# Decayed attention and a gated convolution on one core: transposes in 64-row tiles, states in two column tiles, and a new order of steps

## The chip, the core and the metric

The kernel runs on one core of one Trainium2 chip. The metric is the device time of one execution in microseconds (us), as the median of several runs. TensorE (PE in the profile, its weight loads PEld), VectorE (DVE), ScalarE (ACT) and GpSimd (POOL) each run their own queue of instructions in order; SyncE (SP) issues most of the DMAs. The engines wait for each other by semaphores.

## What is computed

For 4 batches of 8 heads, 768 positions and head size 48, a complex decay runs along the sequence; its output, with the heads put side by side (384 columns), goes through a gate from a convolution of five taps and two matrix products. All is in float32.

```python
for t in range(S):
    new_re = ar * S_re - ai * S_im          # ar, ai: decay of step t, magnitude at most 0.999
    new_im = ar * S_im + ai * S_re
    S_re, S_im = new_re + k[t] (x) v[t], new_im
    y[t] = q[t] @ S_re
gate = sigmoid(sum over 5 taps of conv_w[k] * x[t - 4 + k])     # x: y of all heads
out = (gate * (x @ w_val)) @ w_out
```

## The kernel before

The kernel turns the recurrence into chunks of 128 positions. ScalarE and VectorE make the running sum of the logarithm of the decay and of its angle, and from these the products `kx` and `qx`: each key and query times cosine and sine of the angle and times a growing or shrinking factor, 96 columns a head. With them a chunk's output is a masked product of queries and keys inside the chunk, plus queries times the state that the chunks before have left.

The work is cut into nine units (`UNITS`): the first batch's first half in two parts of 2 and 6 heads, then a unit for every half (384 positions) of all 8 heads of a batch. What a unit goes through, with the letter of each step:

- `a` to `p`: the chain on ScalarE and VectorE that makes angles and factors. `q` makes the key product (two instructions on VectorE, L473 and L477; `kx` has one buffer), `r` the query product.
- `K` stores `kx` to DRAM (`kd`), `N` reads it back as `kn`, with positions on the partitions, for the states. Both are DMAs on SP's queue.
- `T` turns keys and queries on TensorE (L526): a matmul against the identity, three of 128 positions each for one head and half, into one PSUM bank. `U` copies a bank to `kT` or `qT` on ScalarE.
- `s` forms scores (L555 to L560), `M` masks them on VectorE (L571), `t` adds a chunk to the states (L593, 4 heads a step), `u` copies the states, `y` forms outputs (L628, L633, L638), `v` copies them (both copies on ScalarE), `X` moves them to `xT` by DMAs that GpSimd issues.
- `C` and `D` are the taps of the convolution (the first on ScalarE, four on VectorE, L691), `G` the gate on ScalarE, `P` the product with `w_val` (L722), `Z` gate times value on VectorE, `O` the product with `w_out` (L729), `Q` its copy on ScalarE, `W` the store.
- `j` and `l` are the offsets (L363, two matmuls of 384 columns in all), `w` and `L` the weights, `A` and `V` the loads, `B` a copy on GpSimd.

The table `ORDER`, a string of these letters, sets the order of all steps: the program calls the generators one letter after the other, and each instruction is tied behind the one before it on its engine. A float32 matmul runs as two passes, so the trace has twice the program's count of them; a transpose runs as one.

A matmul that writes only partitions 0 to 63 or 64 to 127 of a bank (scores: 64 weight columns; outputs: 48) takes a column tile of TensorE's array, and a matmul of the other half can go beside it. Transposes, states, offsets and `P` and `O` took the full array. Four PSUM banks (`mm`) serve `T`, `P`, `O`, `j` and `l`.

Behind the tiled part lies a step-by-step version of the recurrence, taken only when a flag says that the factors left the safe range; in these runs it isn't.

Of the kernel before, what the change touches and what calls it, by code (L numbers as in the profile page):

```python
# [10 lines left out]
F32 = mybir.dt.float32  # L11
# [14 lines left out]
BUFS = {'in': 4, 'v': 2, 'kn': 2, 'xT': 2, 'z': 2, 'lv': 2, 'an': 2, 'tmp': 2, 'qx': 2, 'kx': 1, 'kT': 6, 'S': 1, 'S_sb': 3, 'S_cr': 4, 'y_sb': 3, 'sm': 2, 'ot': 2, 'mm': 4, 'y': 1}  # L26
XSTEP = 2
PIN_SP = True
POOLQ = 'X'
TAP0 = 'act'  # L30
ORDER = (
    "AAVLaaAbcceafgadiibclmhhdcwjwwwhhjwkknpewpBfkkwwoVgqArowqriinooTTBAaAaUAlmpbUpTUqATUrKcdqTUTLwssANtr"
    "TaTTuAhMMyhacUjwUUbsvceyvkcMskseBfnKtugfMigTdiyvtuilwooilshympAAANtmvMuTThqUUqtujUUtuprMTrUTTtyTuVUU"
    "UTTTvysMpkUtvTpsMkUsTautaUyuAbUMTvTKUAqUAcywTTvyNcUUsesUMMsrvTntfXXyoouwvgUTMdTtyUUXvTTiUXutqBUAhATr"
    "AhiATwauyUwLUalmpjtsskTTpTvMMbUUsUywcMvkTTcUUwTUyvTXTunTewyUTTqUsTUUwvosoMsyrMwMXvXKNtuATTUfUyvqgBUX"
    "UrPituTXCDDTTtyUUKUuNasMstTTaUiulvDsUyCmXCMTCMtCvCCDPputypGZCUDACvuPtdhTTuhtUTUTCGybUUssjutPvkwXMysk"
    "wPGcuZZZdhtTMMnovoyTUTTZAAqOcrvyqhQXeUTTUTUTUTXXUTUUUTjvUsfAAsrMyaMsvkayMPukvyVOnboBvgcWZKUoNiilmXXX"
    "DXtDuTDCCCOUtQDWTTTDQTAAutUTUUUssDDUcOMWDDupTpMOOrtQTWQTyCCqGWUvsAQDuydMvTUUtuUTTTAAtUqKrhPhGGPyeaUU"
    "sTvjNaZTUMyfubZcgBkPPPkZviiltZXZVmssMydnooTAXpTMTutvyBchqWUTUTUTUTeUUUUTTTUfqOKsspMgMiivysvyhutQUUTr"
    "TTvUMTUlmuAyUUvssMyMrvpsMyvTTjUTTpUUUXXNtuXXkkTTTUtUunPZotuTTqTyBUUUssMMTToTvysvyqUUArrKNUUtuTUTTtuO"  # L40
    "vQXMyUUsvsMyMvsMyvTTtuTTUUUtuUTTtUTTTutUyUUssUXvCDMyvMsyCXCCuvTUMTTCCUUTUtWWPTTTUCyuCUUssXMMvyvCDDDD"
    "CsMyEPvOOQQXWWXOQWGZXXPPPGZGZZZPtODCOOuCDDDDDCCQWDDDDCZQWQWyGvXOQWPZGEEGOQWOQWOCQPPZDCZOOCCCGDQDDDWG"
    "QWXCCPZPPCCCGOZZOOOQWQWWQQWW"
# [9 lines left out]
def kernel(  # L53
# [233 lines left out]
    def mm():  # L287
        return ps.tile([P, 512], F32, name="mm", bufs=BUFS["mm"])
# [3 lines left out]
    def weights():  # L292
        cw_row = const.tile([TAPS * NT, P], F32, name="cw_row")
# [287 lines left out]
    def states():  # L581
        for i, (u, n, rs) in enumerate(chunks):
# [6 lines left out]
            for r in rs:  # L589
                for w in range(2):  # L590
                    h = r + w * (g // 2)
                    at = ((n % HN) * g + h) * C2
                    pe(nc.tensor.matmul(  # L593
                        S_ps[bank(u, rs)][:C2, (2 * (h0 + r) + w) * D:(2 * (h0 + r) + w + 1) * D], kn[:, at:at + C2],
                        v_b[b][:, head(u, h), n],
                        start=(i == firsts[bank(u, rs)] and r == rs[0] and w == 0), stop=(n == NCH - 2),
                        skip_group_check=True,
                    ))
# [226 lines left out]
    def step_by_step():  # L825
# [7 lines left out]
        with ExitStack() as es:  # L833
# [13 lines left out]
            with tc.For_i(0, S, TB) as t0:  # L847
                tl = {}
                for nm, src in (("ar", a_re), ("ai", a_im), ("k", k), ("q", q), ("v", v)):
# [56 lines left out]
                for b in range(B):  # L906
                    nc.sync.dma_start(
                        out=xd[b, ds(t0, TB), :].rearrange("t (h e) -> h t e", e=D), in_=yo[b * H:(b + 1) * H]
                    )
            with tc.For_i(0, B, 1) as b:  # L910
                xn = sp.tile([P, J, DM], F32, name="xn")
                nc.sync.dma_start(out=xn, in_=xd[ds(b, 1)].rearrange("o (p j) c -> (o p) j c", j=J))
# [13 lines left out]
                for t0 in (0, HS):  # L926
# [5 lines left out]
                    for m in range(t0, t0 + HS, P):  # L932
# [4 lines left out]
                        nc.sync.dma_start(out=out[ds(b, 1), m:m + P].rearrange("o p c -> (o p) c"), in_=ot)  # L937
# [32 lines left out]
```

## Time and profile before

| | before |
|---|---|
| median of 3 runs | 320.6 us (316.15 to 323.51) |
| profiled execution | 317.13 us |
| its span, from the first to the last instruction | 315.4 us |
| TensorE, VectorE, ScalarE busy | 275.7, 240.7, 239.1 us |
| TensorE's mean granted clock | 0.982 |

The span is what the trace covers; the execution is a little longer. Busy times are unions of the instructions' own times. Matmuls are pipelined: one takes about 0.25 us from start to end while others start behind it every 0.1 us, so busy is not the same as at its peak.

### The profile page before, as it was taken

The numbers are of one execution on the slowest core, as the hardware profiler recorded it, in microseconds if no ns is written. First come the engines' busy times: TensorE is split into PE (matmuls) and PEld (weight loads), VectorE is DVE, ScalarE is ACT, GpSimd is POOL, SyncE is SP. The second block draws the span as 40 slices with busy tenths as digits, with TensorE's granted clock in tenths as the row PEclk, the third lists the DMA queues.
The fourth block names the chain that finished last, engine by engine and source line by source line (L and its number), as shares of the span: only waits on it lengthen the run. The fifth ranks groups of instructions, "written<-read, shape, count | busy, mean of one in ns | idle before, by whom it ended". The sixth has DMA issues, their size and how long they took to land.

```text
span 315.4 us, 7175 instructions
## 1 busy us (share of the span) xinstructions
PE 275.7 (87%) x2887; PEld 211.5 (67%) x2887; DVE 240.7 (76%) x289; ACT 239.1 (76%) x429; POOL 63.4 (20%) x124
## 2 busy tenths in 40 slices
PE   0342959987899999999999999999998999999992
PEld 0121646876687888787778668898898875655551
DVE  4978989997999999999799996983823692281730
ACT  6999989998899999999999899579445515333211
POOL 6410001132017000643400302331333020030000
PEclk9999987997999999999999999999999999999999
DMA  7999999699579498998269698792582012042111
GB/s 185 197 261 316 331 208 172 216 267 279 147 253 224 181 237 214 194 226 240 57 191 271 238 211 146 239 231 60 188 189 72 22 38 77 0 137 76 52 48 58
DMA packets 73748, 54.80 MB, mean 174 GB/s; under 512 B 28511, under 2 KB 70766, under 8 KB 72814
## 3 DMA queue, kind: packets, MB, share of 16 engines
q1 hardware_dynamic: 71150, 49.57, 62.1%
q0 software_dynamic: 2560, 4.72, 6.2%
q8 instruction: 24, 0.39, 0.5%
q14 instruction: 14, 0.11, 0.1%
HBM read 35.40 MB, written 14.16 MB: 157 GB/s over the span
## 4 chain that ended last, share of the span: by engine, by line
PE 58%; ACT 17%; DVE 10%; DMA 9%; issue 2%; SPq 1%; POOL 0%; DVEq 0%; ACTq 0%; POOLq 0%
PE mm L722 14%; PE mm L729 14%; PE mm L526 8%; PE S_ps L593 5%; DMA kn<-kd 5%; PE y_ps L628 4%; DMA kd<-kx 3%; PE sc_ps L555 3%; DVE kx L477 3%; ACT tmp L147 3%; ACT L145 3%; ACT qx L147 2%; PE y_ps L633 2%; PE y_ps L638 2%; ACT lv L147 2%
## 5 line engine op out<-in xcount | busy, mean ns | idle before, releaser
L157 POOL DMA_DIRECT2D xT<-y_sb x80 | 40.3, 510 | 148.3 <-ACT y_sb L150 115.6
L691 DVE SCALAR_TENSOR_TENSOR z<-xT,cw_sb,z 128x768 f32<-128x768 f32 (+1 forms) x60 | 50.4, 862 | 8.3 <-ACT z L147 6.7
L722 PE MATMUL mm<-xT,w_sb 128*128 128x384 f32 x144 | 49.9, 493 | 0.0
L729 PE MATMUL mm<-w_sb,z 128*128 128x384 f32 x144 | 49.2, 491 | 0.0
L571 DVE TENSOR_TENSOR sm<-sc_ps,mask 128x384 f32<-128x384 f32 (+1 forms) x51 | 26.5, 527 | 19.4 <-PE sc_ps L560 16.7
L593 PEld LDWEIGHTS S_ps<-v_in,kn 128*96 128x96 f32 x320 | 33.3, 170 | 9.9 <-issue 5.3
L593 PE MATMUL S_ps<-v_in,kn 128*96 128x48 f32 x320 | 35.1, 251 | 4.2 <-DMA kn<-kd 3.2
L729 PEld LDWEIGHTS mm<-w_sb,z 128*128 128x128 f32 x144 | 26.6, 190 | 16.8
L722 PEld LDWEIGHTS mm<-xT,w_sb 128*128 128x128 f32 x144 | 26.5, 190 | 16.6
L526 PE MATMUL mm<-ident,kx 128*96 128x128 f32 x192 | 30.3, 293 | 8.0 <-DVE kx L477 8.0
L556 PE MATMUL sc_ps<-qT,kT 96*64 96x128 f32 x192 | 37.0, 289 | 0.0
L555 PE MATMUL sc_ps<-qT,kT 96*64 96x128 f32 x192 | 36.5, 287 | 0.5 <-DVE sm L571 0.5
L150 ACT COPY qT<-mm 96x384 f32<-96x384 f32 x64 | 27.8, 494 | 5.4 <-PE y_ps L628 3.0
L145 ACT ACT_TABLE_LOAD x24 | 30.8, 1283 | 1.2 <-PEq L954 0.8
L150 ACT COPY y_sb<-y_ps 112x256 f32<-112x256 f32 (+1 forms) x51 | 18.7, 367 | 16.0 <-PE y_ps L638 15.8
L526 PEld LDWEIGHTS mm<-ident,kx 128*96 128x96 f32 x192 | 21.7, 136 | 11.3 <-issue 9.1
L150 ACT COPY kT<-mm 96x384 f32<-96x384 f32 x64 | 28.8, 487 | 0.3
L526 PE MATMUL mm<-ident,qx 128*96 128x128 f32 x192 | 28.0, 285 | 0.5 <-DVE lv L443 0.5
L557 PE MATMUL sc_ps<-qT,kT 96*64 96x64 f32 x192 | 27.5, 226 | 0.0
L150 ACT COPY ot<-mm 128x384 f32<-128x384 f32 x24 | 11.1, 475 | 21.6 <-PE mm L729 14.6
L560 PE MATMUL sc_ps<-qT,kT 96*64 96x64 f32 x192 | 27.4, 225 | 0.0
L746 DVE TENSOR_TENSOR z<-mm,z 128x384 f32<-128x384 f32 x24 | 13.0, 551 | 18.2 <-PE mm L722 12.0
(90 smaller groups left out, 590.9 us busy)
## 6 DMA issues: line engine op xcount, KB each, us to landing
kd<-kx SPq DMA_DIRECT2D x7, 1152.0 KB, 5.2
out_dram<-ot SPq DMA_DIRECT2D x24, 192.0 KB, 1.9
ar_in<-in_a_re_dram SPq DMA_DIRECT2D x7, 576.0 KB, 7.5
ai_in<-in_a_im_dram SPq DMA_DIRECT2D x7, 576.0 KB, 6.8
k_in<-in_k_dram SPq DMA_DIRECT2D x7, 576.0 KB, 8.4
q_in<-in_q_dram SPq DMA_DIRECT2D x7, 576.0 KB, 9.1
kn<-kd SPq DMA_DIRECT2D x7, 576.0 KB, 4.5
kn<-kd SPq DMA_DIRECT2D x14, 288.0 KB, 6.2
```

The source lines that it names most:

```text
L145: turn("act", nc.scalar.preload_act_table_set(sets[0]))
L150: return turn("act", nc.scalar.copy(out, in_))
L157: ins = (nc.gpsimd if pool else nc.sync).dma_start(**kw)
L526: pe(nc.tensor.transpose(pt[:C2, j, :], src[:, j, f, h, :], ident))
L555: pe(nc.tensor.matmul(lo[:, :C], part(u, 0, ha, n, 0, HC), part(u, 1, ha, n), start=True, stop=True))
L556: pe(nc.tensor.matmul(hi[:, 0::2], part(u, 0, hb, n, 0, HC), qb, start=True, stop=True))
L557: pe(nc.tensor.matmul(lo[:, C:], part(u, 0, hb, n, HC, C), part(u, 1, hb, n, HC, C), start=True, stop=True))
L560: pe(nc.tensor.matmul(hi[:, 1], part(u, 0, ha, n, HC, C), part(u, 1, ha, n, HC, C), start=True, stop=True))
L593: pe(nc.tensor.matmul(S_ps[bank(u, rs)][:C2, (2 * (h0 + r) + w) * D:(2 * (h0 + r) + w + 1) * D], kn[:, at:at + C2], v_b[b][:, head(u, h), ...
L691: dve(nc.vector.scalar_tensor_tensor(out=z, in0=xT[:, c, EXT + t0 - t:EXT + t0 - t + n], scalar=cw_sb[:, TAPS - 1 - t, c:c + 1], in1=z, op ...
L722: pe(nc.tensor.matmul(pv[:, :n], wv_sb[:, ci, c * P:(c + 1) * P], xT[:, ci, EXT + t0:EXT + t0 + n], start=(ci == 0), stop=(ci == NT - 1),))
L729: pe(nc.tensor.matmul(po[:, :DM], z[:, ci, m:m + P], wo_sb[:, ci, :], start=(ci == 0), stop=(ci == NT - 1)))
```

## The change

`T` now turns two heads in one step and cuts each transpose at partition 64: the first 64 positions of each block of 128 go to one PSUM bank, the last 64 to another, each as a matmul of 64 rows against a 64x64 part of the identity. `U` still copies one bank at a time. `t` writes each head's 96 state rows as two matmuls of 64 weight columns, to partitions 0 to 63 and 64 to 127; so that the last head has 128 columns to read, `kn` gets 32 more columns, which GpSimd clears. `cw_row` shares a buffer with the outputs. The DMAs of the branch that isn't taken go to GpSimd's queue. The table `ORDER` is new throughout; it has 64 `T` where it had 128.

```diff
-BUFS = {... 'kx': 1, 'kT': 6, 'S': 1, 'S_sb': 3, ...}
+BUFS = {... 'kx': 1, 'kT': 3, 'S': 1, 'S_sb': 3, ...}
...
 ORDER = (
-    "AAVLaaAbcceafgadiibclmhhdcwjwwwhhjwkknpewpBfkkwwoVgqArowqriinooTTBAaAaUAlmpbUpTUqATUrKcdqTUTLwssANtr"
+    "aAAabAcceafgiabVBdhhcdicLwlmVBhBpjkkhenpwjkfoowknoqgiilwoqTAAmpwrArTaAUKUAAqqawTpUsUbsUrrcMTNyUsMKLt"
...
     def load_kn(u, f):
-        flat = tl[u]["kn", f] = sb.tile([C, HN * g * C2], F32, name="kn", bufs=BUFS["kn"])
-        kn = flat.rearrange("i (n h c) -> i n h c", n=HN, h=g)
+        flat = tl[u]["kn", f] = sb.tile([C, HN * g * C2 + C - C2], F32, name="kn", bufs=BUFS["kn"])
+        pool(nc.gpsimd.memset(flat[:, HN * g * C2:], 0.0))
+        kn = flat[:, :HN * g * C2].rearrange("i (n h c) -> i n h c", n=HN, h=g)
...
     def weights():
-        cw_row = const.tile([TAPS * NT, P], F32, name="cw_row")
+        cw_row = sb.tile([TAPS * NT, P], F32, name="cw_row", tag="ot", bufs=BUFS["ot"])
...
     def flips():
                 for f in range(nf):
-                    for h in [r + w * (g // 2) for r in rs for w in range(2)]:
-                        pt = mm().rearrange("p (j x) -> p j x", j=4)
-                        for j in range(JH):
-                            pe(nc.tensor.transpose(pt[:C2, j, :], src[:, j, f, h, :], ident))
-                        pts.append((u, s, f0 + f, h, pt))
+                    for r in rs:
+                        pt = [mm()[:C2, :2 * JH * HC].rearrange("c (w j p) -> c w j p", w=2, j=JH) for _ in range(2)]
+                        for w in range(2):
+                            for j in range(JH):
+                                for o in range(2):
+                                    at = slice(o * HC, (o + 1) * HC)
+                                    pe(nc.tensor.transpose(
+                                        pt[o][:, w, j, :], src[at, j, f, r + w * (g // 2), :], ident[at, at]
+                                    ))
+                        pts.append((u, s, f0 + f, r, pt))
                         yield

     def flip_copies():
         while True:
-            u, s, f, h, pt = pts.pop(0)
-            t = sb.tile([C2, HS], F32, name=("kT", "qT")[s], bufs=BUFS["kT"])
-            act_copy(t.rearrange("c (p j) -> c p j", j=JH), pt[:C2, :JH].rearrange("c j p -> c p j"))
-            tl[u]["T", s, f, h] = t
-            yield
+            u, s, f, r, pt = pts.pop(0)
+            b, h0, g, f0, nf = units[u]
+            t = sb.tile([C2, 2, HS], F32, name=("kT", "qT")[s], bufs=BUFS["kT"])
+            for w in range(2):
+                tl[u]["T", s, f, r + w * (g // 2)] = t[:, w]
+            for o in range(2):
+                act_copy(
+                    t[:, :, o * HS // 2:(o + 1) * HS // 2].rearrange("c w (p j) -> c w p j", j=JH),
+                    pt[o].rearrange("c w j p -> c w p j"),
+                )
+                yield
...
     def states():
-                    pe(nc.tensor.matmul(
-                        S_ps[bank(u, rs)][:C2, (2 * (h0 + r) + w) * D:(2 * (h0 + r) + w + 1) * D], kn[:, at:at + C2],
-                        v_b[b][:, head(u, h), n],
+                    for lo in (0, HC):
+                        pe(nc.tensor.matmul(
+                            S_ps[bank(u, rs)][lo:lo + HC, (2 * (h0 + r) + w) * D:(2 * (h0 + r) + w + 1) * D],
+                            kn[:, at + lo:at + lo + HC], v_b[b][:, head(u, h), n],
...
-                        nc.sync.dma_start(out=t[w * BH:(w + 1) * BH], in_=view[:, ds(t0, TB), cols])
+                        nc.gpsimd.dma_start(out=t[w * BH:(w + 1) * BH], in_=view[:, ds(t0, TB), cols])
```

The order shows this on TensorE. In the middle of the program before (rows 351 to 357 of its queue), state steps (L593) and transposes (L526) alternate with output products (L729), all on the full array:

```order
L593 MATMUL S_ps<-v_in,kn 96x48 x4
L526 MATMUL mm<-ident,kx 96x128 x3
L729 MATMUL mm<-w_sb,z 128x384 x3
L593 MATMUL S_ps<-v_in,kn 96x48 x4
L526 MATMUL mm<-ident,qx 96x128 x12
L593 MATMUL S_ps<-v_in,kn 96x48 x4
L526 MATMUL mm<-ident,kx 96x128 x3
```

Now, at a like place (rows 338 to 344; L641, L646 and L651 are the outputs, L530 the transposes, L606 the states):

```order
L641 MATMUL y_ps_106<-qT,S_sb 48x128 x4
L646 MATMUL y_ps_106<-sm,v_in 48x64 x4
L651 MATMUL y_ps_106<-sm,v_lo_102 48x64 x4
L530 MATMUL mm<-ident,qx 96x64 x12
L606 MATMUL S_ps<-v_in,kn 64x48 x8
L530 MATMUL mm<-ident,qx 96x64 x12
L530 MATMUL mm<-ident,kx 96x64 x12
```

A step of transposes is 12 matmuls of 64 columns where two steps were six of 128, a state step 8 where it was 4, and the borders between kinds that need another tiling have moved to the transposes.

At the end of TensorE's queue before, from the last output step on (L638 is its last part, L722 the value products, L729 the output products, L509 the flag):

```order
L638 MATMUL y_ps_106<-sm,v_lo_103 48x64 x4
L729 MATMUL mm<-w_sb,z 128x384 x3
L722 MATMUL mm<-xT,w_sb 128x384 x3
L509 MATMUL mm<-ones,hits 1x1
L729 MATMUL mm<-w_sb,z 128x384 x9
L722 MATMUL mm<-xT,w_sb 128x384 x6
L729 MATMUL mm<-w_sb,z 128x384 x6
L722 MATMUL mm<-xT,w_sb 128x384 x9
L729 MATMUL mm<-w_sb,z 128x384 x12
```

And now (L651 the last part of the last output step, L735 the value products, L742 the output products):

```order
L651 MATMUL y_ps_106<-sm,v_lo_103 48x64 x4
L735 MATMUL mm<-xT,w_sb 128x384 x3
L742 MATMUL mm<-w_sb,z 128x384 x3
L735 MATMUL mm<-xT,w_sb 128x384 x9
L742 MATMUL mm<-w_sb,z 128x384 x15
L735 MATMUL mm<-xT,w_sb 128x384 x6
L742 MATMUL mm<-w_sb,z 128x384 x3
L735 MATMUL mm<-xT,w_sb 128x384 x6
L742 MATMUL mm<-w_sb,z 128x384 x6
L735 MATMUL mm<-xT,w_sb 128x384 x3
L742 MATMUL mm<-w_sb,z 128x384 x9
```

Behind the last output step stood 48 of these products and now stand 63 (two passes each in the trace): they have moved towards the end.

## Rows read from the trace of the kernel before

**Rows 1.** The page's head and busy times.
```profile
span 315.4 us, 7175 instructions
...
PE 275.7 (87%) x2887; PEld 211.5 (67%) x2887; DVE 240.7 (76%) x289; ACT 239.1 (76%) x429; POOL 63.4 (20%) x124
```

**Rows 2.** Windows: stretch, busy time and count by engine, clock, DMA share, GB/s.
```profile
0.00:198.30 198.30, 165.73 (x1807) 129.37 (x1809) 180.32 (x204) 187.62 (x315) 44.58 (x85) 0.97 0.89 217
198.30:223.80 25.50, 25.32 (x416) 22.75 (x411) 18.55 (x21) 18.21 (x41) 8.85 (x18) 1.00 0.68 171
223.80:309.50 85.70, 84.59 (x673) 59.42 (x671) 41.78 (x65) 32.80 (x74) 10.00 (x21) 1.00 0.26 81
```

**Rows 3.** Chain of waits, in order of time: start us, us, what.
```profile
146.89 2.13 PE mm L722 x6
...
221.23 2.57 DVE kx L477
223.81 5.63 DMA kd<-kx
...
230.54 6.79 DMA kn<-kd
...
301.79 7.75 PE mm L729 x24
```

**Rows 4.** Timeline of TensorE near 121 us: start us, us, engine, line.
```profile
120.58 0.88 PE L593 MATMUL S_ps<-v_in,kn 128*96 128x48 f32 x8
121.30 0.82 PE L526 MATMUL mm<-ident,qx 128*96 128x128 f32 x6
121.96 0.80 PE L593 MATMUL S_ps<-v_in,kn 128*96 128x48 f32 x8
122.60 0.82 PE L526 MATMUL mm<-ident,qx 128*96 128x128 f32 x6
123.35 0.65 PE L628 MATMUL y_ps<-qT,S_sb 96*48 96x128 f32 x8
```

**Rows 5.** Timeline of TensorE near 190 us.
```profile
189.38 0.61 PE L628 MATMUL y_ps<-qT,S_sb 96*48 96x128 f32 x8
189.82 0.40 PE L633 MATMUL y_ps<-sm,v_in 128*48 128x64 f32 x8
190.05 0.39 PE L638 MATMUL y_ps<-sm,v_lo 128*48 128x64 f32 x8
190.37 0.86 PE L526 MATMUL mm<-ident,kx 128*96 128x128 f32 x6
```

**Rows 6.** Groups by line and shape: busy us, mean ns, idle before.
```profile
L145 ACT ACT_TABLE_LOAD x24 | 30.8, 1283 | 1.2 <-PEq L954 0.8
...
L150 ACT COPY kT<-mm 96x384 f32<-96x384 f32 x64 | 28.8, 487 | 0.3
...
L150 ACT COPY y_sb<-y_ps 112x256 f32<-112x256 f32 x45 | 17.1, 381 | 14.5 <-PE y_ps L638 14.3
...
L150 ACT COPY ot<-mm 128x384 f32<-128x384 f32 x24 | 11.1, 475 | 21.6 <-PE mm L729 14.6 <-DMA out_dram<-ot 3.5 <-issue 3.5
...
L147 ACT ACTIVATE tmp<-lv,b_inv 128x1152 f32<-128x1152 f32 x7 | 9.0, 1286 | 0.0
...
L147 ACT ACTIVATE z<-z 128x768 f32<-128x768 f32 x9 | 7.3, 854 | 0.0
...
L665 POOL MEMSET xT<- 128x12 f32 x4 | 0.8, 194 | 23.8 <-issue 23.6
```

**Rows 7.** Who waited for whom, whole run, GpSimd: us, times, longest us.
```profile
POOL xT L157 <- ACT y_sb L150: 115.6, 12, 24.7
```

**Rows 8.** The same up to 198.3 us, ScalarE.
```profile
ACT y_sb L150 <- PE y_ps L638: 3.8, 4, 1.5
ACT lv L147 <- DVE qx L477: 1.6, 2, 1.1
...
ACT ot L150 <- PE mm L729: 0.8, 1, 0.8
```

More of the change, by code (lines that the diff above doesn't have):

```diff
@@ L25 @@
 GROUPWISE = True
-BUFS = {'in': 4, 'v': 2, 'kn': 2, 'xT': 2, 'z': 2, 'lv': 2, 'an': 2, 'tmp': 2, 'qx': 2, 'kx': 1, 'kT': 6, 'S': 1, 'S_sb': 3, 'S_cr': 4, 'y_sb': 3, 'sm': 2, 'ot': 2, 'mm': 4, 'y': 1}
+BUFS = {'in': 4, 'v': 2, 'kn': 2, 'xT': 2, 'z': 2, 'lv': 2, 'an': 2, 'tmp': 2, 'qx': 2, 'kx': 1, 'kT': 3, 'S': 1, 'S_sb': 3, 'S_cr': 4, 'y_sb': 3, 'sm': 2, 'ot': 2, 'mm': 4, 'y': 1}
 XSTEP = 2
@@ L29 @@
 POOLQ = 'X'
+ROWT = True
 TAP0 = 'act'
 ORDER = (
-    "AAVLaaAbcceafgadiibclmhhdcwjwwwhhjwkknpewpBfkkwwoVgqArowqriinooTTBAaAaUAlmpbUpTUqATUrKcdqTUTLwssANtr"
[L33 to L41, printed above, removed]
@@ L42 @@
-    "CsMyEPvOOQQXWWXOQWGZXXPPPGZGZZZPtODCOOuCDDDDDCCQWDDDDCZQWQWyGvXOQWPZGEEGOQWOQWOCQPPZDCZOOCCCGDQDDDWG"
-    "QWXCCPZPPCCCGOZZOOOQWQWWQQWW"
+    "aAAabAcceafgiabVBdhhcdicLwlmVBhBpjkkhenpwjkfoowknoqgiilwoqTAAmpwrArTaAUKUAAqqawTpUsUbsUrrcMTNyUsMKLt"
+    "TAceAaUsUfwgiutdMaviwwuhAhUAlwUjmpkNbkATTUUpynvoowwqyMturTsMAqsKcUdtUhUrThutcajevXXuytakbvAUfkTUgyuc"
+    "MsivycenvUMstfMdiuoyvlgimAoisUMtuTwyvhhUtUUuTlNjyXpwUtpvmUTsXkskqXpUTAuMsyUTMwUrvtUUUyqXpTTMvunVrAqy"
+    "LBUUUsvsUtKauatMuwosMyvXXTUwwwTyUUUvAbcoTMTyUwUUrwvdXsMTcNqsMyvstutUUUuyhtefruvTUTMAAAyUUsUsCaXvDtga"
@@ new lines @@
+    "hKNMujTUiMwiltukyCvbTAAAsUUUTmTCctyUcUvpTDCkMyUXCUUTBuevqtnpussMsrfoUUtuyMoUDPTDGDMtGgqvZrdhUuhaPyva"
+    "PUyVCtKXAviiZANTUUlbscCmsMMCTuCycUeUsMvpTUXyvXXXpjkfCGrUZPZPZydTvXUkUtwuTTUUUAsAqhBAMtnuDDhoDOQOQsWW"
+    "oDDTyUqrvsUMXCGjOKUPZaVtuyaTvUUQWkkBtuNPbMycctZTUgTUUsMisiMutesvydlXhmvnMOhyTCUoQWTvyUUUUTUvTCCCUssM"
+    "UojMADukpkPTyqvtqusMtyUUTDUDOprUUTXXvuGZtyUsUsMutvyTQTsvUUuMyrMTUUDDTvyUXXXUUsPGMAZAUsBsBTTfgiivyXKN"
+    "tnUOUOouUlWUmQPMMZOQWtvyopTqQqTutWKpNvUyUXuUUtsMrrPPZvXOyXCDTZQuTUtsUsvUuMyUTTvUDMDUtuCWyUUssMvyXXDM"
@@ L44 @@
+    "tusMTTEvyUUUtUvCTTutyUUUsUsvMXutuyMsvyPCCCCECCCvDMWOOGQOWGGQPQPWWDCCCyZPZZOQEZPZPPZvWDXOQWOODDXXDGZD"
+    "CCGOODDDQDGWQWQWQCPZPZODDQCCCCDDDGCCCCCPZPGOOGZPZOOWQOWQWQWQWQWW"
 )
@@ L592, in states @@
                     at = ((n % HN) * g + h) * C2
-                    pe(nc.tensor.matmul(
-                        S_ps[bank(u, rs)][:C2, (2 * (h0 + r) + w) * D:(2 * (h0 + r) + w + 1) * D], kn[:, at:at + C2],
-                        v_b[b][:, head(u, h), n],
-                        start=(i == firsts[bank(u, rs)] and r == rs[0] and w == 0), stop=(n == NCH - 2),
-                        skip_group_check=True,
-                    ))
+                    for lo in (0, HC):
+                        pe(nc.tensor.matmul(
+                            S_ps[bank(u, rs)][lo:lo + HC, (2 * (h0 + r) + w) * D:(2 * (h0 + r) + w + 1) * D],
+                            kn[:, at + lo:at + lo + HC], v_b[b][:, head(u, h), n],
+                            start=(i == firsts[bank(u, rs)] and r == rs[0] and w == 0), stop=(n == NCH - 2),
+                            skip_group_check=True,
+                        ))
             yield
@@ L906, in step_by_step @@
                 for b in range(B):
-                    nc.sync.dma_start(
+                    nc.gpsimd.dma_start(
                         out=xd[b, ds(t0, TB), :].rearrange("t (h e) -> h t e", e=D), in_=yo[b * H:(b + 1) * H]
@@ L911, in step_by_step @@
                 xn = sp.tile([P, J, DM], F32, name="xn")
-                nc.sync.dma_start(out=xn, in_=xd[ds(b, 1)].rearrange("o (p j) c -> (o p) j c", j=J))
+                nc.gpsimd.dma_start(out=xn, in_=xd[ds(b, 1)].rearrange("o (p j) c -> (o p) j c", j=J))
                 xT = sp.tile([P, NT, EXT + S], F32, name="sxT")
@@ L936, in step_by_step @@
                         nc.scalar.copy(ot, po[:, :DM])
-                        nc.sync.dma_start(out=out[ds(b, 1), m:m + P].rearrange("o p c -> (o p) c"), in_=ot)
+                        nc.gpsimd.dma_start(out=out[ds(b, 1), m:m + P].rearrange("o p c -> (o p) c"), in_=ot)
     with tc.If(outside > 0):
```

## The prediction, made before the changed kernel was run

> **What bounds the kernel now.** The page of the profile comes first: of the 315.4 us TensorE is busy 87%, VectorE and ScalarE 76% each [rows 1]. Such a share hides two stages, so I cut the run where the key products of the last two units end, since a unit's keys can be turned, stored and read back only from there. Up to the eighth product (198.3 us) ScalarE is busy 187.6 us, 94.6%, and VectorE 180.3; behind the ninth (223.8) ScalarE works 32.8 of 85.7 us and TensorE 84.6 [rows 2]. The chain of waits says the same: from 146 us on it is TensorE almost alone, broken once by the last product and its way through DRAM (221 to 237 us), in which TensorE has other work, and it ends in 24 output matmuls at 323 ns each [rows 3]. So two clocks set the end: when the eighth product is made, which is ScalarE's load plus what it waits, and how much TensorE has left from there. The last output matmul ends at 309.5; the span is 5.9 us longer, the execution (317.1) 1.7 longer still, and the median of the runs (320.6) stands at 1.011 of this execution.
>
> **What a TensorE step takes.** A matmul's own time (some 270 ns) is its latency; what counts is the pace, from the start of one run of equal matmuls to the start of the next, over the count. Six transposes: 121.30 to 121.96, 110 ns each. Eight state matmuls: 0.64 us in one run and 0.72 in the run before, so 80 and 90 ns; I take 85. They stream 48 columns only, so it is the load of their 96 weight columns that sets this pace. Outputs and scores run in pairs, one in each 64-column tile: four pairs of 128 columns take 0.44 us (110 ns a pair), four of 64 columns 0.23 (57). A change of tiling costs about 0.1 us: six transposes with outputs behind them hold TensorE for 0.75 us where 0.66 is their pace, and four output pairs with transposes behind them for 0.32 where it is 0.23 [rows 4, 5].
>
> **The change part by part.** *Transposes.* 384 full ones become 384 pairs of 64 rows, each with a load of 96 weight columns and 64 columns to stream. No row shows two row tiles. If the streaming limits, a pair takes 57 ns; if the load limits as in the states, 85; if the two loads follow each other, 170. I take 85, since the weights keep their 96 columns, and since the paired outputs show two loads at once. 384 x (110 - 85) = 9.6 us less.
>
> The Trainium skill (TensorEngine Tiling, "The Solution" and "Theoretical Speedup") gives a contraction of at most 64 rows up to twice the speed; a pair would then take 55 ns, an estimate from 110, and the whole sum would fall by another 11.5 us. The state row speaks against the full factor.
>
> *States.* 320 matmuls become 320 pairs with 64 weight columns each. Load-bound they take 85 x 64/96 = 57 ns, the same as the 64-column output pairs; the other end is 85. I take 57: 9.0 us less.
>
> *Tiling changes.* States now share the column tiles of scores and outputs, transposes have a tiling of their own. Counted in the table, neighbours of different tiling rise from 88 to 122: 34 x 0.1 = 3.4 us more, if a change from row to column tiles costs what one from full to column tiles does (ends: nothing, and double).
>
> The same page ("Key Properties") says that any change of mode drains the array, so it puts this price on all 122. The trace agrees for the kind it has: the 0.09 us twice above.
>
> Sum for TensorE over the whole run: 15.2 us less.
>
> *Copies.* A copy still moves 96x384 values (487 ns), and there are 128 as before [rows 6]; the buffers are half as many and twice as big. No difference. *Padding.* Nine clears of 32 columns on GpSimd, 0.2 us each like the clears of xT; what is queued behind them is the issue of xT pieces, and GpSimd waits 115.6 us for those anyway [rows 6, 7]. Each clear waits for a free kn buffer, as the read into it does, so the states behind it wait no longer. If that cover failed, 9 x 0.2 = 1.8 us. *The rest:* cw_row in a shared buffer is used once at the start; the DMAs moved to GpSimd lie in the branch that isn't run.
>
> **The order.** Because two clocks set the end, the saving counts only as far as it lies behind the eighth product or brings that product forward. Counted in the table (step letters), TensorE has left behind it, before: 36 T (0.33), 12 t (0.68), 18 s (0.67), 18 y (0.90), 31 P and O (1.94), 2 offsets (0.65), 16 tiling changes: 11.9 + 8.2 + 12.0 + 16.1 + 60.1 + 1.3 + 1.6 = 111.2 us. (A score step has four pairs of 128 columns and four of 64, an output step four and eight.) The trace has 309.5 - 198.3 = 111.2, so the paces hold. After: 18 T (6 x 0.085 = 0.51), 13 t (8 x 0.057 = 0.46), 16 s, 17 y, 36 P and O, 1 offset, 29 changes: 9.2 + 5.9 + 10.7 + 15.2 + 69.8 + 0.7 + 2.9 = 114.4 us. So 3.2 us more are left, not less: five of the value and projection steps that stood ahead of the cut stand behind it. All of the saving, and more, lies in front, where ScalarE sets the pace.
>
> How much earlier is the eighth product? ScalarE's work up to it changes by one key copy (-0.5), two output copies (+0.8), two row copies (-0.95), two gates (-1.7) and one inverse (-1.3): -3.7 us [rows 6], with as many table loads (one state copy fewer is left out). Its waits for TensorE up to there are 3.8 + 0.8 = 4.6 us; the wait for VectorE (1.6) stays [rows 8]. A faster TensorE can take away between none and all of the 4.6; with nothing to tell, I take half, 2.3. The product then ends at 198.3 - 3.7 - 2.3 = 192.3. Three more table loads come behind the cut (1.28 each, 3.8 us [rows 6]); ScalarE has 50 us to spare there, which hides them; on the path they would be 3.8.
>
> End of TensorE 192.3 + 114.4 = 306.7; span 312.6; execution 314.3; on the scale of the median x 1.011 = **317.8 us**, 0.9% below. A measurement of this kernel can tell about 2% from no change, so this counts as none.
>
> **The rivals.** *All of the slack is taken.* ScalarE waits no longer for TensorE (190.0) and a transposing pair takes 57 ns, so 18 x 6 x 0.028 = 3.0 us less is left (111.4). The end is 301.4, the time 312.4; and if the changes of tiling between row and column tiles cost nothing, 2.5 us less, near 310. For it: in the paired outputs load and streaming overlap fully. Against it: ScalarE would be busy 183.9 of 190.0 us, 97%. Chance 0.31, and it decides from a pair of 60 ns.
>
> *Two row tiles don't load together.* At 170 ns a pair the 18 steps left cost 9.2 us more (123.6), and the 46 ahead cost 23.5 more, which takes away all that the states saved there, so ScalarE keeps its waits: 194.6 + 123.6 = 318.2, the time 329. It is slower by over 2% from 150 ns a pair. For it: no row shows a load in a row tile. Against: loads of two column tiles do go together. Chance 0.12.
>
> *A step takes two of the four PSUM banks at once* where it took one, and value, projection and offset steps hold the others. If each of the 18 steps left waits for one more copy (0.49 us), that is 8.8 us, and those ahead leave ScalarE its waits: 194.6 + 123.2 = 317.8, the time 329. Against it: a step and its two copies move as much per bank as before. Chance 0.08.
>
> *The change doesn't do what it says for the end*: the eighth product comes where ScalarE's load alone puts it (194.6), and 114.4 us are left: 309.0, the time 320.2. This lies within the forecast's own range.
>
> **How the numbers follow.** Forecast with its no-change end 0.49 (314 to 322), the fast rival 0.31, the two slow ones 0.20. The range leaves out the slow rivals in their full size and the lowest part of the fast one: 308 to 327. Faster by over 2% (below 314.2) takes the fast rival and a little of the forecast: 0.33. Slower by over 2% (above 327.0) takes the slow rivals but for a part in which their price is met on fewer steps: 0.16. Within 2%: 0.51.
>
> **What would show it.** In the profile of the changed kernel: a pair of transposes at 85 ns start to start (57 or 170 is a rival); state pairs at 57; 0.1 us at each row-column border; the eighth key product near 192 us and some 114 us of TensorE behind it, with hardly a gap. It is wrong if TensorE has long waits behind the eighth product, or if that product comes before 187 or after 198 us.

## The result, and the profile of the changed kernel

The changed kernel takes 306.15 us (median of 4 runs, 305.97 to 306.95) against 319.93 for the kernel before (4 runs, 316.15 to 323.51): a ratio of 0.961, 95% interval 0.952 to 0.970. It is 4% faster, where no change was forecast, and it lies below the forecast's range. Medians in this document are over all executions of a kernel; the ratios leave out those that took over 1.5% longer than its fastest one.

The page of the changed kernel (head, busy time with instruction counts, ScalarE's busy tenths, granted clock, chain by engine) answers to [rows 1]:

```profile
span 304.5 us, 8598 instructions
...
PE 254.2 (83%) x3591; PEld 188.7 (62%) x3591; DVE 240.5 (79%) x289; ACT 242.0 (79%) x432; POOL 65.2 (21%) x133
...
ACT  6999999999999999999999999789935655014221
...
PEclk9999995599999999999999999999999999999999
...
PE 46%; ACT 24%; DVE 22%; issue 5%; DMA 1%; POOL 0%; ACTq 0%; DVEq 0%; POOLq 0%
```

TensorE works 21.5 us less than in [rows 1], VectorE the same and ScalarE 2.9 us more. In the chain that ended last TensorE has 46% of the span, where the page of the kernel before gives it 58%; until about 165 us that chain runs through ScalarE and VectorE. So the first stage is theirs now, and TensorE has room in it.

The same windows as in [rows 2], cut where the eighth and the ninth key product end (191.1 and 219.7 us) and where TensorE ends (300.7):

```profile
0.00:191.10 191.10, 145.77 (x2371) 112.53 (x2372) 177.78 (x202) 185.32 (x317) 45.52 (x95) 0.96 0.93 231
191.10:219.70 28.60, 28.60 (x493) 22.33 (x493) 20.50 (x22) 25.62 (x49) 9.61 (x16) 1.00 0.44 125
219.70:300.70 81.00, 79.81 (x736) 53.82 (x732) 42.18 (x67) 30.59 (x68) 10.11 (x22) 1.00 0.27 84
```

The eighth product comes 7.2 us earlier (198.3 before), and ScalarE is busy 97% of the time up to it (94.6% before). Behind it TensorE has 109.6 us (111.2 before), all but 1.2 of them busy.

ScalarE's waits up to that product, answering to [rows 8]:

```profile
ACT lv L147 <- DMA ar_in<-in_a_re_dram: 1.1, 1, 1.1
ACT L145 <- PEq L967: 1.0, 1, 1.0
ACT lv L147 <- DVE qx L478: 0.9, 2, 0.6
...
ACT qT L150 <- PE mm L530: 0.2, 1, 0.2
```

Of the 4.6 us that ScalarE waited for TensorE, 0.2 are left.

TensorE's timeline near 199 us, with two transposing steps in a row and the output step behind them:

```profile
199.11 0.88 PE L530 MATMUL mm<-ident,qx 64*96 64x64 f32 x24
199.91 0.64 PE L641 MATMUL y_ps<-qT,S_sb 96*48 96x128 f32 x8
```

Twelve pairs take 0.80 us from the first start to the next operation's; the single records show 3 to 5 ns within a pair and 51 to 53 ns to the next, with about 0.13 us more at the two ends, so a pair is paced at 56 ns. A pair of states takes 58 ns. Going from the column tiles to the row tiles or back costs 0.09 us each time, and the first pair behind it some 0.04 more.

The end of the chain of waits, answering to [rows 3]:

```profile
294.94 5.82 PE mm L742 x18
300.82 0.48 ACT ot L150
```

The last matmul ends at 300.7 and the span 3.8 us later; before it was 5.9.

### The profile page after: what moved, and what is told of

It reads as the page before. It is cut to its first block, busy times and chain, and to the rows that moved or that the text cites. A ratio compares the mean times of both kernels' runs of the same rounds, so it can differ in the third digit from the quotient of the medians.

```text
span 304.5 us, 8598 instructions
## 1 busy us (share of the span) xinstructions
PE 254.2 (83%) x3591; PEld 188.7 (62%) x3591; DVE 240.5 (79%) x289; ACT 242.0 (79%) x432; POOL 65.2 (21%) x133
## 4 chain that ended last, share of the span: by engine, by line
PE 46%; ACT 24%; DVE 22%; issue 5%; DMA 1%; POOL 0%; ACTq 0%; DVEq 0%; POOLq 0%
PE mm L742 14%; PE mm L735 12%; ACT tmp L147 5%; ACT L145 4%; ACT an L147 4%; PE mm L530 4%; DVE qx L478 4%; DVE kx L478 3%; PE S_ps L606 3%; PE sc_ps L567 3%; PE y_ps L641 3%; ACT qx L147 3%; ACT lv L147 2%; DVE z L704 2%; DVE sm L583 2%
## 5 line engine op out<-in xcount | busy, mean ns | idle before, releaser
L704 DVE SCALAR_TENSOR_TENSOR z<-xT,cw_sb,z 128x768 f32<-128x768 f32 (+1 forms) x60 | 51.8, 874 | 6.1 <-ACT z L147 4.6
L735 PE MATMUL mm<-xT,w_sb 128*128 128x384 f32 x144 | 50.1, 492 | 0.4 <-ACT kT L150 0.3
L742 PE MATMUL mm<-w_sb,z 128*128 128x384 f32 x144 | 49.0, 489 | 0.0
L567 PE MATMUL sc_ps<-qT,kT 96*64 96x128 f32 x192 | 37.4, 291 | 2.2 <-ACT qT L150 1.5
L742 PEld LDWEIGHTS mm<-w_sb,z 128*128 128x128 f32 x144 | 27.0, 190 | 18.2
L735 PEld LDWEIGHTS mm<-xT,w_sb 128*128 128x128 f32 x144 | 26.6, 190 | 18.2 <-DVE an L431 0.5
L568 PE MATMUL sc_ps<-qT,kT 96*64 96x128 f32 x192 | 37.5, 291 | 0.0
L606 PE MATMUL S_ps<-v_in,kn 128*64 128x48 f32 x640 | 27.9, 230 | 4.0 <-ACT S_sb L150 3.9
L606 PEld LDWEIGHTS S_ps<-v_in,kn 128*64 128x64 f32 x640 | 23.8, 144 | 7.4 <-ACT S_sb L150 5.2
L569 PE MATMUL sc_ps<-qT,kT 96*64 96x64 f32 x192 | 27.9, 228 | 0.0
L572 PE MATMUL sc_ps<-qT,kT 96*64 96x64 f32 x192 | 27.8, 228 | 0.0
L641 PE MATMUL y_ps<-qT,S_sb 96*48 96x128 f32 x256 | 21.3, 286 | 6.4 <-ACT y_sb L150 5.9
L569 PEld LDWEIGHTS sc_ps<-qT,kT 96*64 96x64 f32 x192 | 25.1, 145 | 0.2 <-issue 0.2
L572 PEld LDWEIGHTS sc_ps<-qT,kT 96*64 96x64 f32 x192 | 25.2, 145 | 0.0
L530 PE MATMUL mm<-ident,kx 64*96 64x64 f32 x384 | 19.7, 239 | 5.1 <-ACT an L147 4.0
```

Source lines behind the costliest of these rows:

```text
L567: pe(nc.tensor.matmul(lo[:, :C], part(u, 0, ha, n, 0, HC), part(u, 1, ha, n), start=True, stop=True))
L568: pe(nc.tensor.matmul(hi[:, 0::2], part(u, 0, hb, n, 0, HC), qb, start=True, stop=True))
L569: pe(nc.tensor.matmul(lo[:, C:], part(u, 0, hb, n, HC, C), part(u, 1, hb, n, HC, C), start=True, stop=True))
L572: pe(nc.tensor.matmul(hi[:, 1], part(u, 0, ha, n, HC, C), part(u, 1, ha, n, HC, C), start=True, stop=True))
L606: pe(nc.tensor.matmul(S_ps[bank(u, rs)][lo:lo + HC, (2 * (h0 + r) + w) * D:(2 * (h0 + r) + w + 1) * D], kn[:, at + lo:at + lo + HC], v_b[b ...
L704: dve(nc.vector.scalar_tensor_tensor(out=z, in0=xT[:, c, EXT + t0 - t:EXT + t0 - t + n], scalar=cw_sb[:, TAPS - 1 - t, c:c + 1], in1=z, op ...
```

## The experiments

Three theories could be told apart by putting each part back. A: the new matmuls bring the gain under any order. B: the order brings it with any matmuls. C: each needs the other. Medians of runs, with the ratio to runs of the kernel before on the same chip:

| | old order | new order |
|---|---|---|
| full transposes, full states | 319.9 to 321.8 (the kernel before) | 323.04, 1.014 [1.006, 1.021] |
| full transposes, states in two column tiles | 320.70, 1.002 [0.997, 1.007] | 315.37, 0.989 [0.982, 0.996] |
| transposes in two row tiles, full states | not run | 314.25, 0.983 [0.974, 0.992] |
| both new | 320.25, 1.006 [1.001, 1.011] | 306.15, 0.961 [0.952, 0.970] |
| old matmuls, last unit's place cleared | 316.64, 0.992 [0.988, 0.997] | |
| both new, last unit's place cleared | 314.15, 0.988 [0.978, 0.998] | |

**The new order with the states as before** (full array, no padding).

```diff
-                    for lo in (0, HC):
-                        pe(nc.tensor.matmul(S_ps[...][lo:lo + HC, ...], kn[:, at + lo:at + lo + HC], ...))
+                    pe(nc.tensor.matmul(S_ps[...][:C2, ...], kn[:, at:at + C2], ...))
```

> The changed kernel with the states as before (one full-array matmul of 96 weight columns a head, no padding of kn); transposes in 64-row tiles and the new order stay. Theory A (cheaper TensorE work is what shortens the run): behind the eighth key product 13 state steps cost 0.68 us where they cost 0.46, 2.8 us more, and 16 more changes of tiling 1.5, and ahead of it ScalarE waits again for a part: 310 to 314 us against 306. Rival B (the new order by itself is the gain): 306 to 308.

314.25 us. In the new order the column-tile states are worth some 7 us by the ratios (0.983 against 0.961), 8.1 by the medians.

**The changed kernel with one row tile written after the other** in each transposing step.

```diff
-                        for w in range(2):
-                            for j in range(JH):
-                                for o in range(2):
+                        for o in range(2):
+                            for w in range(2):
+                                for j in range(JH):
```

> The changed kernel with the twelve transposes of a step written tile by tile: six in the upper 64 rows, then six in the lower, so that no two run side by side; nothing else moves. If a single 64-row transpose is paced by its 64 columns (some 56 ns) a step takes 0.67 us, what two steps of before took, and the undone part is just the side-by-side run: theory A 313 to 318 us (18 steps behind the eighth key product, 0.33 us each, and ScalarE's waits back). If it is paced by the load of 96 weight columns (85 ns) a step takes 1.0 us and the time is above 320. Rival B: below 309.

309.19 us, ratio 0.973 [0.966, 0.980]: only 3.0 us of loss. A step near 142 us:

```profile
141.67 0.70 PE L530 MATMUL mm<-ident,kx 64*96 64x64 f32 x12
142.29 0.65 PE L641 MATMUL y_ps<-qT,S_sb 96*48 96x128 f32 x8
```

It takes 0.62 us to the next operation's start. Six pairs take 0.47 in the changed kernel (141.36 to 141.83), and twelve one after the other at 56 ns, with 0.13 at the ends, would take 0.80. The single records show why. A step's first matmuls, all of one row tile, start 56 ns apart, so one 64-row transpose with its 96 weight columns needs no more than that. From the third on, starts 47 to 49 and 7 to 9 ns apart follow: the two row tiles run side by side although they are written one after the other, and where two steps adjoin (qx and kx), matmuls of the one and of the other start in turn. So this edit took the pairs away only in part.

**The new order, with one row tile after the other and full states.** The two edits above together.

> The new order alone, with TensorE's work as dear as before: transposes one tile at a time and states on the full array. Theory A: nothing is gained over the kernel before, 317 to 325 us. Rival B: most of the gain is there, 305 to 311.

316.44 us, ratio 0.992 [0.988, 0.996]. After what the run above showed, this isn't the order alone; that follows further down.

**The old order with both new matmuls.** A transposing step now holds two heads, so of every two T of the old table the second stays, and copies that would have no data yet go right behind it.

```diff
-    ...UTTTvysMpkUtvTpsMkUsTautaUyuAbUMTvTKUAqUAcywTTvyNcUU...
+    ...UTvysMpkUtvTpsMkUsautaUyuAbUMTvKUAqUAcywTvyNcUU...
```

> The new transposes and states in the order of before; only each second letter T now stands for a step of two heads, and the copies that would come ahead of it are moved right behind it. Theory A: behind the eighth key product 105 us of TensorE work are left where 111 were, and the product comes up to 5 us earlier: 306 to 312 us, so the matmuls alone bring most of the gain. Rival B: 315 to 321, no gain without the order.

320.25 us: no gain, though by the paces above TensorE has 24 us less to do than in the kernel before (29.4 less in matmuls, 5.5 more in 55 more changes of tiling). Theory A falls.

**The new order with full transposes** (two heads a step; six copies moved ahead of score steps that need them), the new states kept.

```diff
-                                for o in range(2):
-                                    at = slice(o * HC, (o + 1) * HC)
-                                    pe(nc.tensor.transpose(pt[o][:, w, j, :], src[at, j, f, ...], ident[at, at]))
+                                pe(nc.tensor.transpose(pt[w][:, j, :], src[:, j, f, ...], ident))
```

> The changed kernel with the transposes back on the full array, two heads a step, one head to a bank; six of the 128 copies are moved ahead of a score step that now needs them; states and the rest of the order stay. A step costs 0.65 us where it costs 0.34. Theory C (the parts pay only together, under an order made for them): 18 steps behind the eighth key product make 5.7 us, and the product comes some 3 us later: 312 to 317 us. Rival (the transposes side by side hardly matter, as the run with one tile at a time seemed to say): 308 to 311.

315.37 us: the side-by-side transposes are worth 9.2 us in the new order.

**The new order alone**: full transposes as in the run before this one, and full states.

> The new order with transposes and states both on the full array, as in the kernel before; six copies moved as in the run above. Nothing of the new tiling is left. Theory C: the order needs the cheaper matmuls, so this is no faster than the kernel before, 318 to 326 us. Rival B (the order is the gain): below 312.

323.04 us, 1.4% slower than the kernel before. Theory B falls. Its windows up to the eighth product and behind it:

```profile
0.00:197.80 197.80, 162.01 (x1855) 128.93 (x1855) 179.02 (x202) 186.40 (x313) 45.06 (x88) 0.96 0.90 223
197.80:317.50 119.70, 119.68 (x1036) 86.55 (x1032) 62.73 (x89) 58.35 (x119) 18.63 (x36) 1.00 0.28 87
```

The new order leaves TensorE 8.5 us more behind the eighth product than the old one, without a gap, and with the old matmuls that product comes no earlier to speak of. The new matmuls then bring it from 197.8 to 191.1 and shorten what is left from 119.7 to 109.6: 16.8 us, against 16.9 between the medians.

**The kernel before with the new states alone.**

> The kernel before with its own order and its own transposes, and only the states in two column tiles with padded keys. Theory C: TensorE saves some 0.2 us a state step, but the old order gives it back as waits: 315 to 320 us, no difference that can be measured. Rival D (the old order gained nothing only since its copies had been moved in that run): the states alone bring 4 us or more, 310 to 316.

320.70 us: nothing. By count it saves 8.6 us of matmuls (320 x 27 ns) and gives back 4.8 in 48 more changes of tiling; behind the eighth product 2.6 and 1.8.

**The changed kernel with the branch's DMAs back on SP** (the branch isn't run).

```diff
-                        nc.gpsimd.dma_start(out=t[...], in_=view[...])
+                        nc.sync.dma_start(out=t[...], in_=view[...])
```

> The changed kernel with the DMAs of the branch that isn't taken back on SP's queue. Behind the last output matmul the changed kernel needs 3.8 us to the end of its span where the kernel before needed 5.9; SP's waits at that branch are the difference in the trace. If the queue of these DMAs is the cause, this run takes 2 us longer at the very end, 308 us; if it isn't, 306.

309.28 us, ratio 0.972 [0.963, 0.981]. TensorE ends at 300.7 in both, but the span is 306.5 instead of 304.5: 2.0 of the 3.1 us between the medians. In the changed kernel SP works off nine of its last semaphore waits (302.2 to 302.8 us) while the last store is on its way and has three behind its landing (303.4); with the DMAs on SP it stands until 304.2 and then does all twenty, one after another.

**The kernel before with those DMAs moved**, the same edit the other way round.

> The kernel before with one thing of the change alone: the DMAs of the branch that isn't run are issued from GpSimd instead of SP. The prediction costed this at nothing. If SP's waits behind the last store belong to those DMAs' queue, the span ends about 3.7 us behind the last output matmul instead of 5.9, as in the changed kernel, whatever the matmuls' own time is. If they belong to the stores, it stays at 5.9.

One execution, 321.0 us. The span (319.4) ends 3.7 us behind the last output matmul (315.7) instead of 5.9, as the first theory of this run had it. That matmul came 6.2 us later than in the trace of before, in a program whose matmuls and order are the same; TensorE waited 2.7 us for the last unit's keys there (1.0 before) and then had half its clock for 10.2 us. First this run, then the kernel before, each with the wait and the window behind it (the two columns behind GpSimd's are clock and DMA share):

```profile
PE S_ps L593 <- DMA kn<-kd: 2.7, 1, 2.7
238.00:249.00 11.00, 9.56 (x97) 9.40 (x99) 1.35 (x3) 3.96 (x8) 2.47 (x5) 0.53 0.10 28
```

```profile
PE S_ps L593 <- DMA kn<-kd: 1.0, 1, 1.0
238.00:249.00 11.00, 11.00 (x168) 9.99 (x168) 7.08 (x9) 7.12 (x16) 2.46 (x5) 1.00 0.12 31
```

The run with the merging alone, below, comes back to that.

**The changed kernel with the six copies moved** as the runs with full transposes had them.

> The changed kernel with six copies of transposed heads moved ahead of the score step behind which they stood, the move that the two runs with full transposes in the new order needed; nothing else. If the gain of the side-by-side transposes in the new order (315.4 to 306.2) is theirs, the move costs at most 1 us: 305.5 to 307.2. If the move itself took part of those 9.2 us, the time is 308 or more, and the gain of the transposes is smaller by that.

306.95 us, ratio 0.956 [0.949, 0.962]. The move costs some 0.8 us, so the 9.2 and 16.9 us above are the matmuls' but for that.

**The 64-row transposes as plain matmuls against the identity.**

```diff
-                                    pe(nc.tensor.transpose(
-                                        pt[o][:, w, j, :], src[...], ident[at, at]
+                                    pe(nc.tensor.matmul(
+                                        pt[o][:, w, j, :], src[...], ident[at, at], start=True, stop=True,
```

> The changed kernel with its 64-row transposes as plain float32 matmuls against the identity (same tiles, same weights of 96 columns, same 64 columns to stream). It asks what was wrong with the 85 ns that the prediction took for a pair from the load of 96 weight columns. If the weight load of a plain matmul is what takes 85 ns for 96 columns and the transposing mode is spared it, a pair is paced at 85 ns here, and TensorE has 18 x 6 x 0.029 = 3 us more behind the eighth product: about 309 to 312. If a row tile of 64 rows loads its weights in half the time in either mode, the pair stays at 56 to 58 ns and the time at 306 to 307.

335.17 us, far above either expectation, because a plain float32 matmul stands in the trace as two instructions where a transpose is one (1536 against 768). The eighth product comes at 207.3 us, 16.2 later, and TensorE needs 13.0 us more behind it. A step of six pairs near 151 us, with the output step behind it:

```profile
151.39 1.24 PE L530 MATMUL mm<-ident,kx 64*96 64x64 f32 x24
152.55 0.42 PE L642 MATMUL y_ps<-qT,S_sb 96*48 96x128 f32 x4
```

Twelve pairs of instructions take 1.16 us, with much the same extra time at the two ends: 85 ns each, starts 7 and 78 ns apart. That is the 85 ns that the prediction took. With tiles of the same size and the same weights a pair of instructions in transposing mode takes 56, and one pair is enough. So the state row was a price for plain matmuls and not for transposes; how the mode loads its weights no run here shows.

**The old order with the merging alone**: two heads a step, full transposes, full states.

> The kernel before with one thing of the change alone: two heads a transposing step, in full 128-row transposes, the two steps of a pair put where the second stood and the copies that this would leave without data put right behind it; states, and all other steps in the old order. TensorE's work is that of before (12 transposes of 110 ns a step, no more changes of tiling). It asks why the new matmuls under the old order brought nothing. If the merging by itself costs what the faster matmuls saved there (ScalarE gets its copies late: in that run it waited some 6 to 7 us for transposes up to the eighth key product, before none), then the time is 325 to 332 and ScalarE waits 6 us or more for transposes up to the eighth product. If merging is free and the old order simply can't use a faster TensorE, the time is that of before, 318 to 322, and ScalarE's waits for transposes stay under 2 us.

(A step of two heads has six transposes, not the twelve of that text.) 322.82 us, ratio 1.005 [1.001, 1.010]: within the second theory's time, though the first theory's wait is there. ScalarE's wait for key transposes up to 200 us, which is no row in the kernel before, and TensorE's at the last unit:

```profile
ACT kT L150 <- PE mm L527: 6.1, 5, 2.4
```

```profile
PE S_ps L597 <- DMA kn<-kd: 2.2, 1, 2.2
```

The eighth product comes at 202.0 us, 3.7 later than in [rows 2]. And TensorE comes to the last unit's keys before they are back. What follows that wait is in the windows around it:

```profile
230.00:238.00 8.00, 7.93 (x134) 6.80 (x133) 3.50 (x5) 2.64 (x8) 2.60 (x6) 1.00 0.55 171
238.00:249.00 11.00, 8.76 (x85) 8.46 (x84) 0.00 (x0) 5.20 (x14) 0.54 (x2) 0.71 0.43 92
```

With a mean of 0.97 in the 7 us behind them, a mean of 0.71 is 6.8 us at half the clock (1.2 GHz). In all five profiled executions of the old order so far TensorE waits there: 1.0 us in the kernel before, 1.2 with the new states alone, 2.2 here, 2.7 with the branch's DMAs moved, 3.3 with both new matmuls; in the last three its clock is then at half for 6.8 to 10.2 us. (The last one is an execution of 328.8 us, where the median is 320.25; it had half the clock once more, for 6.8 us from 221 us on.) Under the new order no run waits for that read, and none has a half-clock stretch from 111 us to its last matmul. So the old order may lose the gain at this place, or ahead of the eighth product, which comes late where two heads are merged: 202.0 us here with the old matmuls, 3.7 later than before, and 199.4 to 204.2 in the three runs with both new ones.

**Two output steps moved ahead of the last unit's states**, under the old order with the old matmuls, and with the new.

```diff
-...MyvTTtuTTUUUtuUTTtUTTTutU...
+...MyvTTWOQtuTTUUUWOQtuUTTtUTTTutU...
```

> The kernel before, in which two output steps (with their copies and stores) that stood later are moved ahead of the second- and third-last state steps before the last unit's first one; 3.9 us of TensorE's work that is ready. In every run of the old order TensorE came to the last unit's keys before they were back from DRAM (waits of 1.0 to 3.3 us in total for that read), and in three of five runs its clock then stood at half for 6.8 to 10.2 us; in no run of the new order was there such a wait, nor a half-clock stretch behind 110 us. If that place is what the old order loses, then here TensorE waits under 0.3 us for that read, no half-clock stretch lies behind 110 us, the runs lie close together (within 4 us, where before's lie within 9), and the median is 315 to 318. If the place is a symptom (the work is the same and the wait only moves), the median is that of before, 319 to 322, with its spread.

> The same move of two output steps in the run that has the new transposes and states under the old order (two heads merged), which took 320.3 us and waited 3.3 us for that read. If that wait and the half clock behind it are what ate the new matmuls' gain, then the waits are gone and the median is 311 to 316, the more so as TensorE had counted 105 us left behind the eighth key product there. If the gain was lost ahead of the eighth product (which came at 204 us instead of 198, ScalarE waiting for merged transposes), the median is 317 to 320, and at most 3 us of the wait come back.

322.64 and 320.82 us, ratios 1.011 [1.001, 1.021] and 1.012 [1.004, 1.020]: no gain. But the wait had only changed its name. In the first of them, ScalarE's row copy and then TensorE:

```profile
239.16 0.48 ACT L150 COPY ot<-mm 128x384 f32<-128x384 f32 x1 [6.45 <-DMA out_dram<-ot]
```

```profile
PE mm L526 <- ACT ot L150: 3.7, 1, 3.7
```

The copy of the first moved step waits for its buffer, which an earlier row's store still holds behind the last key reads in SP's queue. In the second TensorE's wait is 3.9 us. The clock falls here too (6.8 us in the one, 3.4 in the other). These runs decide nothing.

**The same with the two stores issued earlier**, one ahead of the last unit's key store and one right behind the copy that it stores.

```diff
-qUUArrKNUUtuTUTTtuOvQXMy...vTTtuTTUUUtuUTT...
+qUUArrWKNUUtuTUTTtuOvQWXMy...vTTOQtuTTUUUOQtuUTT...
```

> The two output steps moved ahead as before, in the kernel before, but with their copies' buffers free: the two stores that hold these buffers are issued earlier too (one ahead of the last unit's key store, one right behind the copy that it stores). In the first try the copy of the first moved step waited 6.5 us for such a store, and TensorE 3.7 us for the copy, so the wait for the keys had only changed its name. Here TensorE should wait under 0.5 us between 228 and 246 us and keep its full clock there. If that place is what the old order loses, the median is 315 to 318 and the runs lie within 4 us; if it is a symptom, 319 to 322.

> The same move with the same two stores in the run that has the new transposes and states under the old order. TensorE should wait under 0.5 us for the last unit's keys or for a copy there. If the wait and the half clock behind it ate the new matmuls' gain, the median is 311 to 316. If the gain was lost ahead of the eighth key product (200 to 204 us here, 191 under the new order), it is 317 to 320.

316.64 us with the old matmuls (ten runs from 314.6 to 319.2) and 314.15 with the new ones, inside the ranges that the first theory gave. The window over the place in the first, and the two stages of the second:

```profile
238.00:249.00 11.00, 11.00 (x171) 10.05 (x170) 3.48 (x5) 6.75 (x18) 2.47 (x5) 1.00 0.23 71
```

```profile
0.00:199.40 199.40, 154.91 (x2305) 114.64 (x2307) 180.33 (x204) 187.36 (x315) 47.48 (x92) 0.99 0.88 216
199.40:307.60 108.20, 106.02 (x1290) 75.04 (x1286) 60.26 (x85) 51.22 (x114) 19.09 (x41) 1.00 0.37 105
```

With no wait there the clock stays whole. The place was worth some 3 us with the old matmuls and 6.1 (320.25 to 314.15, and their intervals don't meet) with the new ones. The 8.0 us that still lie between this kernel's median and the changed one's (6.9 between the profiled executions) are ahead of the eighth product: it comes at 199.4 instead of 191.1, while behind it TensorE needs 1.4 us less. Up to there ScalarE has 2.0 us more to do (187.4 against 185.3), and it stands idle 12.0 us instead of 5.8, of which 5.1 are this row:

```profile
ACT kT L150 <- PE mm L530: 5.1, 5, 2.3
```

It is the row that merging alone brought. Theory C stands: the new matmuls need an order made for them. For one place that is shown with its price: TensorE must have other work until the last keys are back. For the other, that two heads should be turned before ScalarE's copies are due, the runs show that merging brings the wait and a later eighth product; but no run takes that wait away under the old order, so how much of the 8.3 us it is worth isn't shown. Nor was a program tried that turns one head in two row tiles and needs no merging.

## Why the prediction was wrong

What bounds the kernel was read rightly: the eighth key product by ScalarE's load and waits, then TensorE almost without a gap. The sum missed by 11.7 us in four terms.

- **The pair of transposes** (the step "I take 85, since the weights keep their 96 columns"). It measured 56 ns, the end named for streaming. On 18 x 6 pairs that is 3.1 us of the 114.4 us forecast behind the eighth product; 109.6 were measured. Where the other 1.7 us come from is shown below. The choice failed because it took the price of a plain matmul's weight load for a transpose: as plain matmuls the same tiles are paced at 85. The factor of up to two that the Trainium skill gives (TensorEngine Tiling (Array Packing), "Theoretical Speedup"), weighed there and set aside, is what the trace shows: 56 for a pair where one full transpose takes 110.
- **Half of ScalarE's waits** ("with nothing to tell, I take half, 2.3"). Of the 4.6 us for TensorE 0.2 were left, and other idle time shrank too: 10.7 us in all before, 5.8 now. The load came down less than counted, by 2.3 instead of 3.7 us: up to the cut ScalarE makes two key copies and two query copies more than before (48 and 46), where the sum had one key copy less. That 192.3 was forecast and 191.1 measured is luck, since the two errors nearly cancel.
- **The DMAs of the branch**, costed at nothing because the branch isn't run. They cost the kernel before 2.1 us at its end (5.9 against 3.7 or 3.8), shown by moving them each way (2.0 and 2.2).
- **The scale of 1.011** from the profiled execution to the median. It was 1.001: 3.3 us. The factor came from the kernel before, whose runs lay between 316 and 324 us. With its last unit's place cleared, the old order's profiled execution took 316.88 us and its median 316.64. What the scale carried over was, at least for its greater part, the wait there and the lower clock behind it, which the run with those DMAs moved shows and the new order doesn't have. The profiled execution of before showed 1.0 us of that wait and no fall of the clock, so it could be read only as a place without slack: keys back at 237.3 us and a state step that starts on them at 236.1.

The four give 1.2 (the eighth product) + 4.8 (TensorE behind it) + 2.1 + 3.3 = 11.4 us, and 0.2 lie between the span and the execution.

Of the 4.8 us behind the eighth product 3.1 are the pairs. TensorE's matmuls from 191.1 us to its last one give most of the rest:

```profile
L567 PE MATMUL sc_ps<-qT,kT 96*64 96x128 f32 x60 | 10.7, 276 | 0.0
L606 PE MATMUL S_ps<-v_in,kn 128*64 128x48 f32 x192 | 7.8, 223 | 0.0
L651 PE MATMUL y_ps<-sm,v_lo 128*48 128x64 f32 x128 | 6.5, 219 | 1.2 <-issue 1.2
L530 PE MATMUL mm<-ident,qx 64*96 64x64 f32 x108 | 4.0, 220 | 0.0
L530 PE MATMUL mm<-ident,kx 64*96 64x64 f32 x96 | 3.5, 219 | 0.0
```

A score step has 4 of L567, a state step 16, an output step 8 of L651, a transposing step 12: that makes 15, 12, 16 and 17 steps, where the table's cut had 16, 13, 17 and 18. By the time of the product TensorE was one step of each kind, and half a product step (213 matmuls are left of 216), further along than the letters ahead of it. At the paces above that is 3.3 us less, and the wait of 1.2 us in the third row, which the sum didn't have, is against it. That makes 5.2 us where 4.8 are missing; 0.4 stay open.

The rival with all of the slack taken was the right one, with the condition that it named (a pair under 60 ns; 56) and its sign against it (ScalarE 97% busy, which it was). It put the last matmul at 301.4 (190.0 + 111.4); it ended at 300.7 (191.1 + 109.6). Its time of 312.4 missed almost by the last two terms alone. The slow rivals fell: two row tiles do load side by side, and transposing steps wait 0.4 us in the whole run for the copies that free their banks. Five more value and projection steps behind the cut were foreseen and are there.

The prices for the state pair (57, measured 58) and a tiling change (0.1; 0.09 and some 0.04 at the first pair) held. Copies and padding were rightly costed at nothing: the nine clears took 1.5 us of GpSimd in all, and no wait row names them.

## What to carry to other kernels

A price is good for its kind of instruction: before a row of another kind sets a bound, look for what differs between the two (here plain matmul and transpose), and leave the chance with the end that it doesn't exclude. Where a faster engine meets an order made for the slower one, ask which transfer or copy it now reaches too early; here the new matmuls brought nothing under the old order, and 6 us came back when one such place was cleared. A cheap test is to move some ready work in there, with the buffers and stores that this work needs. A ratio between median and profiled execution belongs to the waits of the kernel that it was taken from.

## What the hardware showed that was not expected

- Matmuls of two row tiles don't keep the order in which they are written: with six of one tile written ahead of six of the other, they start in pairs 7 to 9 ns apart from the third on (the step at 141.67 us), and where two steps adjoin, matmuls of the one and of the other start in turn (150.66 to 150.78 us in the same run).
- A 64-row transpose with 96 weight columns is paced at 56 ns alone and at 56 ns as a pair of two tiles; as plain matmul instructions the pair takes 85, and there are two of them.
- In the five profiled executions in which TensorE waited 2.2 to 3.9 us for key reads or a copy at the last unit, its clock then stood at half (1.2 GHz) for 3.4 to 10.2 us, and was back at 2.4 GHz after that. In those in which it waited 0 to 1.2 us there, it stayed at 2.4 GHz.
- DMAs that are never run can lengthen the end of the kernel: written on SP's queue they made it 2.0 to 2.2 us longer than on GpSimd's. No run leaves them out.
